# Additive attention masks of the first query block: eight made together on GpSimd, where two were made at each first use

## The chip, the cores and the metric

The kernel runs on one core of one Trainium2 chip. The metric is the device time of one execution in microseconds (us); the kernel before takes 581.28 us, the median of three runs (581.21 to 581.45).

## The reference

Attention over 2 batches, 8 heads, 768 positions and head size 64, followed by two mixture layers on 1536 tokens. Only the attention is touched here. A key is kept for a query when it is one of the first `n_global` (8) positions, or lies at most `n_local` - 1 (95) positions back. A kept key gets a bias that falls with its distance, by a slope of its own for each head:

```python
rel = pos[:, None] - pos[None, :]
is_global = pos[None, :] < int(n_global)
is_local = (rel >= 0) & (rel < int(n_local))
keep = is_global | is_local
dist = np.where(is_global & ~is_local, float(n_local), np.abs(rel).astype(np.float32))
slopes = 2.0 ** (-8.0 * (np.arange(H, dtype=np.float32) + 1) / H)
scores = scores + (-slopes[:, None, None] * dist[None, :, :])[None]
scores = np.where(keep, scores, -1000000000.0)
```

Softmax over the keys and the product with V follow, then `max(x@w1, x@w2, x@w3) @ w_out`, a root-mean-square norm, and `(silu(xn@w_gate) * (xn@w_val)) @ w_out`.

## The kernel before, in words

The attention goes over chunks of two query blocks (a block is 128 queries), and in each chunk over four pairs of heads. A chunk and a pair of heads are a **unit**; 2 x 3 chunks by 4 pairs give 24 units. A query block looks at a window of 232 keys: 96 before it, the 8 global ones, and its own 128. The first query block of a batch has nothing before it and looks at its own 128 keys alone. So there are two widths of mask: narrow (128x128, only for a batch's first query block) and wide (128x232, for all others), each for 8 heads. All depend on a head by one factor, so class `Masks` first makes a common operand for each width on VectorE (lines 706 to 709, tile `mask_mm`, the narrow one first), and each head's mask is that operand times the head's factor, in bf16 (tiles `bias128` and `bias232`, line 715). The first use of a mask makes it, narrow ones on GpSimd, wide ones on VectorE; later units find it made.

`steps` goes over the units with a lead of three: in one step TensorE computes the scores of unit d+3 (line 766), then transposes the weights of unit d+1 (line 807), then multiplies those of unit d with V (line 830), with small filler matmuls in between in the first steps (line 369). For the scores of a unit, `exponents` issues for each query block and each of the two heads a reduction on VectorE (line 779) that adds the mask to the scores, writes the sum and keeps its row minimum, and an exponential on ScalarE (line 783) with its row sum. `normalise` takes the reciprocal of the sums on VectorE (lines 791, 792) and scales the weights on GpSimd (line 797, four instructions a unit).

In the part of the program in which this happens the order on TensorE, VectorE, ScalarE and GpSimd is that in which the code issues the instructions (`manual(FRONT)`); each engine runs its own queue in order. In a step `normalise` of a unit is issued ahead of `exponents` of the next one, and a mask that does not yet exist is issued where `exponents` asks for it:

```python
do(self.normalise, j + LEAD - 1)
do(self.out, j - 1, True)
do(self.scores, j + LEAD)
do(self.transposes, j + 1)
do(self.turned, j + 1, 0)
do(self.exponents, j + LEAD, 0)
```

The score banks have one buffer (`scp`, bufs=1), so the scores of a unit are computed when the reductions of the unit before have read theirs. Transfers are issued by SP's queue. The mixture layers follow; their weights are loaded and split (lines 127 to 168) beside the attention.

Of the kernel before, what the change touches and what calls it, by code (L numbers as in the profile page):

```python
# [13 lines left out]
ALU = mybir.AluOpType  # L14
PSUM = bass.MemoryType.PSUM

P = 128
B, H, S, D = 2, 8, 768, 64
# [11 lines left out]
WIN = NPREV + NG + P  # L30
# [33 lines left out]
SLOPES = [2.0 ** (-8.0 * (h + 1) / H) for h in range(H)]  # L64
# [3 lines left out]
class Later:  # L68
# [3 lines left out]
    def __init__(self):  # L72
        self.now, self.queue = 0, {}

    def __call__(self, steps, fn, *args):
        self.queue.setdefault(self.now + steps, []).append((fn, args))
# [604 lines left out]
class Masks:  # L681
# [3 lines left out]
    def __init__(self, tc, ctx, nlf, ngf):  # L685
        nc = self.nc = tc.nc
        pool = ctx.enter_context(tc.tile_pool(name="mk", bufs=1, side="right"))
        self.out = {n: pool.tile([P, H, n], BF16, name=f"bias{n}") for n in (P, WIN)}
        self.made = set()
        own = NPREV + NG  # L690
        rd = pool.tile([P, 2, WIN], F32, tag="rd", name="mask_rd")
        mm = pool.tile([P, WIN + P], F32, tag="mm", name="mask_mm")
        cg = pool.tile([P, 2, NG], F32, tag="cg", name="mask_cg")
        rel = rd[:, 0]

        kw = {"allow_small_or_imprecise_dtypes": True}
        nc.gpsimd.iota(rel[:, own:], [[-1, P]], base=0, channel_multiplier=1, **kw)
        nc.gpsimd.affine_select(
            rel[:, own:], rel[:, own:], [[-1, P]], ALU.is_ge, FAR, base=0, channel_multiplier=1
        )  # L700
        nc.gpsimd.iota(cg[:, 0], [[1, NG]], base=0, channel_multiplier=0, **kw)
        nc.gpsimd.iota(rel[:, :NPREV], [[-1, NPREV]], base=NPREV, channel_multiplier=1, **kw)
        nc.gpsimd.memset(rel[:, NPREV:own], FAR)
        for n, o in ((P, own), (WIN, 0)):
            m = mm[:, WIN:] if n == P else mm[:, :WIN]
            nc.vector.tensor_scalar(m, rel[:, o:], nlf, MASKED, op0=ALU.is_ge, op1=ALU.mult)
            g = m[:, :NG] if n == P else m[:, NPREV:own]
            nc.vector.scalar_tensor_tensor(out=g, in0=cg[:, 0], scalar=ngf, in1=g, op0=ALU.is_ge, op1=ALU.mult)
            nc.vector.scalar_tensor_tensor(out=m, in0=rel[:, o:], scalar=nlf, in1=m, op0=ALU.min, op1=ALU.add)
        self.parts = {P: mm[:, WIN:], WIN: mm[:, :WIN]}  # L710

    def __call__(self, n, h):
        if (n, h) not in self.made:
            eng = self.nc.gpsimd if n == P else self.nc.vector
            eng.tensor_scalar(self.out[n][:, h, :], self.parts[n], -8.0 * SLOPES[h], 1.0, op0=ALU.mult, op1=ALU.mult)
            self.made.add((n, h))
        return self.out[n][:, h, :]


# [411 lines left out]
```

## Time and profile before

| | |
|---|---|
| median of 3 runs | 581.28 us (581.21 to 581.45) |
| the profiled execution's own time | 581.86 us |
| its span, first to last instruction | 580.0 us |
| TensorE busy | 563.5 us, 97% of the span, 3316 matmuls |
| VectorE busy | 379.6 us, 65% |
| ScalarE busy | 250.9 us, 43% |
| GpSimd busy | 243.2 us, 42%, 301 instructions |
| mean granted clock of TensorE | 0.987 of full speed |

How to read it: the profile records one execution, 1.86 us of whose time lie outside the span. A busy share says how long an engine worked, not whether the end depends on it; that is read from the waits and from the chain of work that ended last. In rows, PE is TensorE, PEld its weight load, DVE VectorE, ACT ScalarE, POOL GpSimd, SP the engine that issues transfers. TensorE's clock has two levels, full (2.4 GHz, shown as 1.00) and half (1.2 GHz, shown as 0.50).

### The profile page before, as it was taken

How to read it: one execution, taken by the hardware profiler on the slowest of the kernel's cores; microseconds unless marked ns; L12 is line 12 of the kernel's file. 1: busy time of each engine (PE TensorE's matmuls, PEld its weight loads, DVE VectorE, ACT ScalarE, POOL GpSimd, SP SyncE). 2: the span in 40 equal slices, each digit the busy share in tenths (PEclk: the TensorE clock that was granted, in tenths of full speed). 3: DMA queues.
4: the chain of work that ended last, by engine and by line, in shares of the span. 5: the costliest groups of instructions: out<-in, count | busy, mean ns of one | idle time of the engine just before them, and what ended most of it. 6: DMA issues, size and time to landing. Idle time of an engine off the chain costs nothing.

```text
span 580.0 us, 9232 instructions
## 1 busy us (share of the span) xinstructions
PE 563.5 (97%) x3316; PEld 510.0 (88%) x3316; DVE 379.6 (65%) x801; ACT 250.9 (43%) x605; POOL 243.2 (42%) x301
## 2 busy tenths in 40 slices
PE   5999999999999999999999999999999999999995
PEld 2677788899999999988899999999999987888884
DVE  4699888826769612156768788888887869762120
ACT  3598676614244201157664444444443435432210
POOL 3456655405145201047647555555565635420000
PEclk9699999999999999999999999999999999999999
DMA  8366655301534400000000222222222104303001
GB/s 301 134 216 199 216 161 180 110 1 49 171 110 152 138 1 0 1 0 2 2 0 1 72 73 74 75 72 73 73 73 73 51 23 146 108 3 127 19 37 42
DMA packets 15895, 48.73 MB, mean 84 GB/s; under 512 B 2016, under 2 KB 2016, under 8 KB 15840
## 3 DMA queue, kind: packets, MB, share of 16 engines
q1 hardware_dynamic: 15840, 48.05, 25.6%
q8 instruction: 28, 0.46, 0.3%
q14 instruction: 27, 0.22, 0.1%
HBM read 44.90 MB, written 3.15 MB: 83 GB/s over the span
## 4 chain that ended last, share of the span: by engine, by line
PE 88%; DVE 5%; ACT 2%; POOL 2%; issue 1%; DMA 1%; SPq 0%; DVEq 0%; POOLq 0%; ACTq 0%
PE q L500 27%; PE mm L379 25%; PE acc L577 16%; PE mo L426 8%; PE sc L766 4%; PE tr L807 3%; PE av L830 3%; ACT s L783 1%; DVE s L779 1%; PE tr L460 1%; DMA qk<-qk 1%; POOL h L550 0%; POOL s L797 0%; POOL op L254 0%; PE idle L369 0%
## 5 line engine op out<-in xcount | busy, mean ns | idle before, releaser
L500 PE MATMUL q<-xb,op 128*128 128x384 f32 x1008 | 175.5, 334 | 0.5 <-POOL op L254 0.5
L500 PEld LDWEIGHTS q<-xb,op 128*128 128x128 f32 x1008 | 174.6, 188 | 0.8 <-POOL op L254 0.8
L379 PE MATMUL mm<-xt,w 128*128 128x384 f32 x864 | 157.5, 338 | 0.0
L379 PEld LDWEIGHTS mm<-xt,w 128*128 128x128 f32 x864 | 148.6, 188 | 2.6 <-issue 2.6
L168 POOL TENSOR_TENSOR w<-x,w 128x512 fp32r<-128x512 f32 x36 | 51.7, 1441 | 74.3 <-ACT w L165 74.2
L797 POOL TENSOR_SCALAR s<-s,rs 128x232 f32<-128x232 f32 (+1 forms) x96 | 43.1, 468 | 42.5 <-DVE rs L792 32.0
L254 POOL TENSOR_TENSOR op<-s,op 128x256 fp32r<-128x256 f32 x48 | 36.9, 781 | 56.7 <-ACT op L253 56.7
L396 DVE TENSOR_TENSOR h<-mm,h 128x384 f32<-128x384 f32 x48 | 26.5, 553 | 46.6 <-PE mm L379 46.4
L426 PE MATMUL mo<-w,rst 128*128 128x512 f32 x216 | 52.1, 395 | 0.0
L783 ACT ACTIVATE s<-s,nmx 128x232 f32<-128x232 f32 (+1 forms) x96 | 44.6, 467 | 15.9 <-DVE nmx L779 15.3
L577 PE MATMUL acc<-w,gst 128*128 128x512 f32 x216 | 49.5, 390 | 1.6 <-POOL w L168 0.8
L577 PEld LDWEIGHTS acc<-w,gst 128*128 128x128 f32 x216 | 40.4, 188 | 10.6 <-POOL w L168 1.2
L577 PE MATMUL acc<-w,st 128*128 128x512 f32 x216 | 49.1, 389 | 0.0
L577 PEld LDWEIGHTS acc<-w,st 128*128 128x128 f32 x216 | 40.5, 188 | 8.4
L426 PEld LDWEIGHTS mo<-w,rst 128*128 128x128 f32 x216 | 39.8, 188 | 8.0
L779 DVE CUSTOM_DVE_ANT_0 s<-sc,bias 128x232 f32<-128x232 f32 (+1 forms) x96 | 32.1, 376 | 12.8 <-PE sc L766 4.6
L517 DVE TENSOR_TENSOR h<-q,h 128x768 f32<-128x768 f32 (+1 forms) x39 | 34.7, 889 | 3.6 <-PE q L500 3.2
L253 ACT CAST op<-s 128x256 fp32r<-128x256 f32 x48 | 18.1, 402 | 41.3 <-DVE s L234 30.8
L766 PE MATMUL sc<-qk 64*128 64x232 f32 (+1 forms) x192 | 28.8, 395 | 7.2 <-DVE nmx L779 6.1
L520 ACT ACTIVATE g<-g 128x768 f32<-128x768 f32 (+1 forms) x26 | 20.8, 798 | 34.8 <-DVE g L517 34.8
L165 ACT CAST w<-x 128x512 fp32r<-128x512 f32 x36 | 22.2, 619 | 26.3 <-DVE x L151 18.0
L766 PEld LDWEIGHTS sc<-qk 64*128 64x128 f32 x192 | 19.0, 202 | 14.2 <-DVE nmx L779 8.3
(102 smaller groups left out, 735.3 us busy)
## 6 DMA issues: line engine op xcount, KB each, us to landing
raw<-wgv SPq DMA_DIRECT2D x24, 512.0 KB, 3.6
raw<-w SPq DMA_DIRECT2D x18, 512.0 KB, 3.8
raw<-wo SPq DMA_DIRECT2D x18, 512.0 KB, 3.6
qk<-qk SPq DMA_DIRECT2D x24, 312.0 KB, 4.0
v<-vwin SPq DMA_DIRECT2D x10, 512.0 KB, 5.1
out<-o SPq DMA_DIRECT2D x12, 256.0 KB, 2.1
v<-vwin SPq DMA_DIRECT2D x2, 256.0 KB, 4.9
gcol<-gcol SPq DMA_DIRECT2D x1, 2.0 KB, 1.6
```

The costliest lines, as they stand in the source:

```text
L168: self.nc.gpsimd.tensor_tensor(out=t[:, 1, :], in0=self.x.pop(i), in1=t[:, 0, :], op=ALU.subtract)
L254: nc.gpsimd.tensor_tensor(out=t[:, 1, :], in0=s, in1=t[:, 0, :], op=ALU.subtract)
L379: self.nc.tensor.matmul(ps, w[:, wi, k * P:(k + 1) * P], x[b][:, k, xi, c0:c0 + C2], start=(i == 0), stop=(i == 3 * KT - 1),)
L396: self.nc.vector.tensor_tensor(out=h, in0=ps, in1=h, op=ALU.max)
L426: self.nc.tensor.matmul(ps, h[:, k % 3, hi, :], w[:, wi, :], start=(k + x == 0), stop=(k == NF1 - 1 and x == 2),)
L500: nc.tensor.matmul(ps, a[:, wi, k * P:(k + 1) * P], self.xb[b][:, j, k, xi, :], start=(i == 0), stop=(i == 5))
L517: nc.vector.tensor_tensor(out=o, in0=ps, in1=x, op=ALU.add)
L577: self.nc.tensor.matmul(ps, of(si), w[:, wi, :], start=(f == LAST[0] and si == 1), stop=(f == LAST[-1] and si == 0 and wi == 0),)
L766: nc.tensor.matmul(sc[j][:, i, :n], qk[r, i * P:(i + 1) * P], qk[r, k0:k0 + n], start=True, stop=True)
L779: nc.vector.tensor_tensor_reduce(out=s[:, j, :n], in0=self.sc[d][j][:, i, :n], in1=self.bias(n, 2 * pr + j), scale=-QK, scalar=3.0e38, op0 ...
L783: nc.scalar.activation(s[:, j, :n], s[:, j, :n], AF.Exp, bias=nmx[:, j:j + 1], scale=-1.0, accum_out=sm[:, i, j:j + 1])
L797: nc.gpsimd.tensor_scalar(s[:, j, :n], s[:, j, :n], rs[:, i, j:j + 1], 1.0, op0=ALU.mult, op1=ALU.mult)
```

## The change

`Masks.__init__` issues all eight narrow masks on GpSimd as soon as the code has issued their common operand, ahead of the wide operand's three instructions. The wide masks are made at their first use on VectorE, as before.

```diff
-        self.made = set()
+        self.made, self.parts = set(), {}
...
             nc.vector.scalar_tensor_tensor(out=m, in0=rel[:, o:], scalar=nlf, in1=m, op0=ALU.min, op1=ALU.add)
-        self.parts = {P: mm[:, WIN:], WIN: mm[:, :WIN]}
+            self.parts[n] = m
+            if n == P:
+                for h in range(H):
+                    self.make(nc.gpsimd, n, h)
+
+    def make(self, eng, n, h):
+        eng.tensor_scalar(self.out[n][:, h, :], self.parts[n], -8.0 * SLOPES[h], 1.0, op0=ALU.mult, op1=ALU.mult)
+        self.made.add((n, h))
 
     def __call__(self, n, h):
         if (n, h) not in self.made:
-            eng = self.nc.gpsimd if n == P else self.nc.vector
-            eng.tensor_scalar(self.out[n][:, h, :], self.parts[n], -8.0 * SLOPES[h], 1.0, op0=ALU.mult, op1=ALU.mult)
-            self.made.add((n, h))
+            self.make(self.nc.vector, n, h)
         return self.out[n][:, h, :]
```

GpSimd's queue from the end of the set-up on, before (`mask_rd` is the distance, `s_0_0` the weights of unit 0 and its first query block, `rs_0` its reciprocals):

```order
L703 MEMSET mask_rd_149 128x8
L715 TENSOR_SCALAR bias128_147<-mask_mm_150 128x128 x2
L797 TENSOR_SCALAR s_0_0_201<-s_0_0_201,rs_0_226 128x128 x2
L797 TENSOR_SCALAR s_0_1_212<-s_0_1_212,rs_0_226 128x232 x2
L715 TENSOR_SCALAR bias128_147<-mask_mm_150 128x128 x2
L797 TENSOR_SCALAR s_1_0_239<-s_1_0_239,rs_1_268 128x128 x2
L797 TENSOR_SCALAR s_1_1_250<-s_1_1_250,rs_1_268 128x232 x2
L715 TENSOR_SCALAR bias128_147<-mask_mm_150 128x128 x2
```

The same place now (lines behind the edit are five higher, and line 715 is 716):

```order
L703 MEMSET mask_rd_149 128x8
L716 TENSOR_SCALAR bias128_147<-mask_mm_150 128x128 x8
L802 TENSOR_SCALAR s_0_0_209<-s_0_0_209,rs_0_232 128x128 x2
L802 TENSOR_SCALAR s_0_1_218<-s_0_1_218,rs_0_232 128x232 x2
L802 TENSOR_SCALAR s_1_0_245<-s_1_0_245,rs_1_272 128x128 x2
L802 TENSOR_SCALAR s_1_1_254<-s_1_1_254,rs_1_272 128x232 x2
```

Three pairs of masks have moved from behind the normalising of units 0, 1 and 2 to the place of the first pair.

VectorE's queue now, from the reciprocal of unit 0 to the second wide mask of unit 1 (rows without an input read out a row minimum; what an instruction waits for stands in brackets):

```order
L797 RECIPROCAL rs_0_232<-rs_0_232 128x4 [waits DVE_49]
L784 ISA s_1_0_245,nmx_1_0_246<-sc0_1_239,bias128_147 128x128 [waits PE_49,Pool_49]
L784 ISA nmx_1_0_246 128x1
L784 ISA s_1_0_245,nmx_1_0_246<-sc1_1_240,bias128_147 128x128 [waits PE_49,Pool_49]
L784 ISA nmx_1_0_246 128x1
L716 TENSOR_SCALAR bias232_148<-mask_mm_150 128x232
L784 ISA s_1_1_254,nmx_1_1_255<-sc0_1_239,bias232_148 128x232 [waits DVE_49]
L784 ISA nmx_1_1_255 128x1
```

Here nothing has moved: the reductions of unit 1 still wait for TensorE and for GpSimd, and the queue reads as before but for line and buffer numbers. So do the queues of ScalarE, TensorE and SP in this part of the program.

## Rows read from the trace of the kernel before

**Rows 1.** Busy time by stretch (start:end, length, each engine's busy us, PEclk, DMA share, GB/s).

```profile
26.00:42.00 16.00, 16.00 (x159) 12.01 (x158) 14.69 (x65) 14.41 (x53) 7.92 (x18) 1.00 0.64 200
```

**Rows 2.** What TensorE waited for, 26 to 60 and 60 to 580: us, times, longest.

```profile
PE sc L766 <- DVE nmx L779: 0.6, 1, 0.6
...
PE acc L577 <- POOL w L168: 0.8, 1, 0.8
```

**Rows 3.** The chain that ended last, 0 to 60: start, us, what.

```profile
10.19 1.60 POOL s L797 x4
11.79 0.28 POOL bias L715
...
13.35 2.20 PE sc L766 x8
15.54 1.47 PE tr L807 x6
17.02 0.23 PE idle L369
...
18.29 2.21 PE sc L766 x8
...
23.99 1.71 PE sc L766 x8
25.70 0.80 PE tr L807 x6
```

**Rows 4.** Timeline: start, us, engine, line, operation, in brackets the idle time before.

```profile
7.63 0.27 DVE L715 TENSOR_SCALAR bias<-mask_mm 128x232 bf16<-128x232 f32 x1
...
9.04 0.88 PE L766 MATMUL sc<-qk 64*128 64x128 f32 x6 [0.15 <-DVE nmx L779]
...
9.84 0.18 DVE L792 RECIPROCAL rs<-rs 128x4 f32<-128x4 f32 x1
...
12.09 0.29 DVE L779 CUSTOM_DVE_ANT_0 s<-sc,bias 128x128 f32<-128x128 f32 x1 [2.08 <-POOL bias L715]
...
14.57 0.17 DVE L791 TENSOR_SCALAR rs<-sm 128x4 f32<-128x4 f32 x1 [0.65 <-ACT s L783]
...
17.03 0.29 DVE L779 CUSTOM_DVE_ANT_0 s<-sc,bias 128x128 f32<-128x128 f32 x1 [2.07 <-PE tr L807]
```

**Rows 5.** GpSimd's timeline from 5 us, and line 797 by form (ns min/median/max).

```profile
6.35 0.70 POOL L715 TENSOR_SCALAR bias<-mask_mm 128x128 bf16<-128x128 f32 x2 [4.01 <-DVE mask_mm L709]
...
16.70 0.57 POOL L715 TENSOR_SCALAR bias<-mask_mm 128x128 bf16<-128x128 f32 x2
...
L715 POOL TENSOR_SCALAR bias<-mask_mm x8: 299/300/317, 6.3 to 22.1; 128x128 bf16<-128x128 f32 x8
L797 POOL TENSOR_SCALAR s<-s,rs x96: 374/462/1141, 10.2 to 114.2; 128x232 f32<-128x232 f32 x80, 128x128 f32<-128x128 f32 x16
```

**Rows 6.** Busy time by stretch again, for the clock (columns as in rows 1).

```profile
10.00:11.60 1.60, 0.24 (x2) 0.00 (x0) 0.01 (x1) 0.00 (x0) 1.41 (x4) 1.00 1.02 415
11.60:13.35 1.75, 0.00 (x1) 0.01 (x1) 1.23 (x8) 0.90 (x5) 0.72 (x3) 0.50 1.03 414
...
18.28:25.20 6.92, 6.92 (x34) 5.24 (x36) 4.38 (x20) 4.37 (x15) 2.20 (x6) 0.50 0.14 47
...
25.20:25.30 0.10, 0.10 (x4) 0.10 (x1) 0.10 (x1) 0.00 (x0) 0.05 (x1) 0.71 0.00 0
```

**Rows 7.** GpSimd and VectorE side by side, at 43.8 and 98.7 us.

```profile
43.78 1.29 POOL L168 TENSOR_TENSOR w<-x,w 128x512 fp32r<-128x512 f32 x1
...
43.95 1.65 DVE L151 SCALAR_TENSOR_TENSOR x<-raw,x 128x512 int32<-128x512 int32 x1
...
98.73 1.82 POOL L797 TENSOR_SCALAR s<-s,rs 128x232 f32<-128x232 f32 x2 [0.44 <-DVE rs L792]
...
99.64 0.67 DVE L145 SCALAR_TENSOR_TENSOR x<-raw,x 128x512 int32<-128x512 int32 x1
```

**Rows 8.** Transfers of q and k, 0 to 40: time to landing.

```profile
DMA to landing us min/median/max: 2.7/4.0/8.1
```

## The prediction

> **What bounds the kernel now.** I read the busy time by stretch first. From 26 us on TensorE works without a gap at the full clock, for instance 16.00 of the 16.00 us from 26 to 42 [rows 1]. Then the list of what TensorE waited for: from 26 us to the end it has one wait of 0.6 us and four that sum to 2.4 us, the longest 0.8 us [rows 2]. (From 42 to 51 us the chain of waits runs through ScalarE and VectorE, but what they do there follows step by step from what came before, so it moves as a whole.) No wait behind 26 us ends at a transfer or at any other event with a time of its own. So the rest of the program moves with its beginning, and what the change is worth is read from the first 26 us alone.
>
> There the chain of waits shows the pattern [rows 3]: GpSimd normalises a unit (four instructions, 1.60 us), then makes a mask (0.28 us), then VectorE's reduction over the scores of the next unit can start, and TensorE's next scores wait for VectorE to empty the score banks. VectorE's own rows show the two waits [rows 4]: 2.08 us before 12.09 and 2.07 us before 17.03. The second is printed as a wait for a transpose; the mask of 16.70 us [rows 5] ends at 16.98, just ahead of 17.03, so it is the mask again. Third, the clock [rows 6]: it falls to 0.50 at 11.60, when TensorE has been idle since 10.24, and comes back at about 25.26 after TensorE has worked without a gap since 18.28. What runs between costs nearly double: six transposes take 1.47 us at the low clock and 0.80 at the high one [rows 3], so each us spent at the low clock costs 0.455 us.
>
> **The change part by part.** I number the units of the first chunk 0 to 3; each has two narrow masks (GpSimd, this change) and two wide ones (VectorE, still made at their first use).
>
> Taken out: three pairs of masks from GpSimd's queue behind the normalising of units 0, 1 and 2. Put in: six masks more behind the first two. A mask is 0.30 us, and followed by another it takes 0.27 to 0.28 of the queue (the pair at 16.70 takes 0.57) [rows 5]. Eight from 6.35 on end by 6.35 + 8 x 0.30 = 8.75, and GpSimd has nothing else until 10.19 [rows 3]: the moved work itself costs nothing, and were that cover gone it would be 6 x 0.28 = 1.7 us. The wait for the first two masks is on the first and second of the eight, in the same place as before, so unit 0 starts at the same time. No transfer moves in any queue, and VectorE, ScalarE, TensorE and SP keep their order.
>
> Term 1, unit 1. VectorE ends its reciprocal at 9.84 + 0.18 = 10.02, and TensorE has the scores ready at 9.04 + 0.88 = 9.92 [rows 4]. The reduction then starts near 10.04 and not at 12.09: **2.05 us earlier**.
>
> Term 2, the wide masks of unit 0. They ran alone in the profile (the first at 7.63, 0.27 us [rows 4]); now GpSimd works beside them until 8.75. No row shows this pair together. The nearest: a VectorE instruction of line 151 whose twin of line 145 takes 0.67 us took 1.65 when it started 0.17 us behind a GpSimd instruction of 1.29 us, that is, it stood until that one was done [rows 7]. So each wide mask waits between nothing and one narrow mask, 0 to 0.30 us; I take the middle, 0.15 each, since the start falls anywhere within a running mask: +0.30 for two (0 to 0.60). They stand on VectorE's path to the reciprocal, so all of it counts.
>
> The Trainium skill, "SBUF — State Buffer", section "Who interferes with whom", says it of a VectorE instruction in a 2-port mode (tensor_scalar can be one) and of one with two SBUF inputs: it and a GpSimd instruction exclude each other for a whole instruction. The trace agrees for line 151. By that rule, with every wide mask caught at the start of a GpSimd instruction, the gain at unit 3 would be the 1.84 us below and not 2.39.
>
> Term 3, the first wide mask of unit 1. Unit 1 now runs beside the normalising of unit 0 (GpSimd instructions of 0.37 to 0.46 us [rows 5]), where before it ran after it: 0 to 0.46, and I take 0.21. The second wide mask there delays only the exponentials (again 0.21).
>
> Scores of unit 2 wait for the third reduction of unit 1, so they start at 13.35 - 2.05 + 0.30 + 0.21 = 11.81. The clock has fallen by then (11.60), so they take the 2.20 us of the row, to 14.01; the transposes of unit 0 follow (1.47, to 15.48), then two filler matmuls of 0.21 each [rows 3]. The transposes need unit 0 normalised: 10.19 + 0.30 + 1.60 + two wide masks of 0.27 in between = 12.6, in time. Scores of unit 3 could start at 15.90, if VectorE is ready: reciprocal of unit 1 at 14.57 - 2.05 + 0.30 + 0.42 = 13.24 [rows 4], reductions of unit 2 from 13.65, the third of them done by 15.05. It is; TensorE is the later. So the scores of unit 3 start at 15.90 where they started at 18.29: **2.39 us earlier**. With no contention at all it is 18.29 - (11.30 + 4.09) = 2.90, about 3.1 with the first 0.3 us at the high clock; with every wide mask waiting a whole GpSimd instruction, 18.29 - (12.36 + 4.09) = 1.84.
>
> From there TensorE has no gap, before and now. The operands are there: the blocks of q and k of units 0 to 3 are the first large transfers in SP's queue, and one takes at most 8.1 us to land [rows 8]; 15.9 leaves nearly twice that. What is late next is TensorE itself.
>
> Term 4, the clock's return, the largest unknown. Its rows are one event, so I bound it by what stood before it. If it comes at the same place in the work (early in the scores of unit 4, 23.99 before), the gain stays 2.4. If it comes after the same length of gapless work (25.26 - 18.28 = 6.98), it comes at 11.81 + 6.98 = 18.8, 4.1 us before that place, and saves 4.1 x 0.455 = 1.85 more: 4.25. If it comes at the same moment, 25.26, the work of 2.4 us runs at the low clock and 2.4 x 0.455 = 1.1 is lost: 1.3. I take 2.8, nearer to the first: the gapless stretch begins earlier now, but with the same short matmuls of the narrow units, and the wide ones still come late in it.
>
> Sum: the profiled execution took 581.86 us, 1.86 more than its span of 580.0; 581.86 - 2.8 = 579.06. The median of the three runs is 581.28, 0.58 lower, so 581.28 - 2.8 = **578.5 us**. The range: 3.1 and 1.85 together give 576.3, rounded to 576.2; 1.84 with the clock at the same moment (1.84 x 0.455 = 0.84 lost) gives 1.0, so 580.3.
>
> **The rivals.** *The clock never falls.* If unit 2's scores begin ahead of 11.60, TensorE's idle time ahead of it shrinks from 1.36 us to 1.0, and the clock may hold. Then TensorE is no longer the bound, but the loop from reduction to reciprocal to the next reduction: 14.57 - 12.09 = 2.48, and 0.4 for the reciprocal and 0.42 for contention, 3.3 a unit. The reductions of unit 4 come at 10.34 + 3 x 3.3 = 20.2, and the scores that they read were done at 25.70 before: 5.5 earlier, 575.8. Against it: by term 2 the scores come after 11.60, when the gap is as long as before. Chance 0.07.
>
> *GpSimd keeps the operands for its whole group.* Then a wide mask waits not for one instruction but for the end of the group. Unit 0 loses 8.75 - 7.63 = 1.12, unit 1 some 1.25, unit 2 some 1.3; scores of unit 2 start at 13.7, those of unit 3 at 17.85, 0.4 before the old time: 580.9, no difference that can be told. Against it: at 99.64 a VectorE instruction of line 145 (two SBUF operands) ran its usual 0.67 us among two of GpSimd's normalising instructions, and these took 1.82 together instead of 2 x 0.46 [rows 5, 7]: it got in between and held up GpSimd. Chance 0.09. Another 0.02 for a gain that is swallowed later by a wait that the profile does not show, and 0.02 for the forecast's own edge below the bound of 0.2%.
>
> *The low clock lasts longer* (the other side). TensorE's gaps move, and the work between 11.8 and 20 us is made of short matmuls; if these do not bring the clock back, each us of delay behind 22.9 costs 0.455. The gain of 2.4 is used up if it returns at 22.9 + 2.4 / 0.455 = 28.2, and the kernel is slower by over 0.2% from 30.8 on. Half as long again as the 13.66 us of before ends at 32.1: 2.4 - 9.2 x 0.455 = -1.8, so 583.1. Against it: work without a gap brought it back in 7 us, and the wide scores of unit 4 come at about 21.6 now. Chance 0.04.
>
> That the change does not do what it says I leave out: the order of GpSimd's queue shows the eight together, and unit 1's first reduction waits for the third of them alone.
>
> **How the numbers follow.** A change of 0.2% is 1.2 us, about what a measurement of this kernel can tell from none. Forecast 0.78, of it 0.76 with a gain above that; faster 0.76 + 0.07 = 0.83, the same 0.09 + 0.02 + 0.02 = 0.13, slower 0.04.
>
> **What would show it.** Right: one row of eight masks on GpSimd from about 6.35 to 9; no wait of VectorE for a mask behind 8 us; the reduction of unit 1 near 10.3, the scores of unit 2 near 11.8 and of unit 3 near 15.9; the wide masks of units 0 and 1 at 0.3 to 0.7 us and not 0.28 throughout; the clock's fall at about 11.6 and its return between 18.8 and 25.3. Wrong: wide masks of over 1 us, a reduction of unit 1 that still starts after 11.5, or a clock that returns after 26.

## The result and the profile after

The changed kernel takes 575.68 us, the median of four runs (575.32 to 576.32), the kernel before beside it 581.35 (581.21 to 581.45): 5.67 us less, a ratio of 0.9904 with a 95% interval of 0.9887 to 0.9921. Faster was forecast, but by 2.8 us, with a range down to 576.2; the time lies 0.5 us below it. A second measurement (after_again below) gave 575.69 against 581.62, 0.9894 (0.9877 to 0.9910). The two profiled executions lie 6.54 us apart, more than the medians: that of the kernel before is 0.5 us above its median, that of the changed one 0.4 below.

| | before | after |
|---|---|---|
| the profiled execution's own time | 581.86 us | 575.32 us |
| its span | 580.0 us | 573.5 us |
| TensorE busy | 563.5 us, 97% | 561.3 us, 98% |

First VectorE's queue after the change: its timeline from 7 to 17 us (start, us, engine, line, operation; in brackets the idle time before and what ended it).

```profile
7.70 0.27 DVE L716 TENSOR_SCALAR bias<-mask_mm 128x232 bf16<-128x232 f32 x1
...
8.33 0.28 DVE L716 TENSOR_SCALAR bias<-mask_mm 128x232 bf16<-128x232 f32 x1
...
10.02 0.29 DVE L784 CUSTOM_DVE_ANT_0 s<-sc,bias 128x128 f32<-128x128 f32 x1
...
10.45 0.31 DVE L716 TENSOR_SCALAR bias<-mask_mm 128x232 bf16<-128x232 f32 x1
...
11.12 0.44 DVE L716 TENSOR_SCALAR bias<-mask_mm 128x232 bf16<-128x232 f32 x1
...
12.97 0.29 DVE L784 CUSTOM_DVE_ANT_0 s<-sc,bias 128x128 f32<-128x128 f32 x1
...
16.48 0.29 DVE L784 CUSTOM_DVE_ANT_0 s<-sc,bias 128x128 f32<-128x128 f32 x1 [0.30 <-PE sc L771]
```

The reductions of units 1, 2 and 3 start at 10.02, 12.97 and 16.48. Before they started at 12.09 and 17.03 [rows 4], and that of unit 3 at 22.09, in a row of the trace of before that the prediction did not use:

```profile
22.09 0.29 DVE L779 CUSTOM_DVE_ANT_0 s<-sc,bias 128x128 f32<-128x128 f32 x1 [2.19 <-POOL bias L715]
```

So there were three waits for a mask, not two, and all three are gone. The lead over the kernel before grows unit by unit: 2.07, 4.06, 5.61 us.

GpSimd after the change (its timeline; the second row is unit 0's normalising):

```profile
6.42 2.73 POOL L716 TENSOR_SCALAR bias<-mask_mm 128x128 bf16<-128x128 f32 x8 [4.08 <-DVE mask_mm L709]
10.26 1.62 POOL L802 TENSOR_SCALAR s<-s,rs 128x128 f32<-128x128 f32 x4 [1.11 <-DVE rs L797]
```

The eight masks stand together and end at 9.15, 1.11 us ahead of the next work.

The clock, by stretches between its changes (start:end, length, busy us and number on PE, PEld, DVE, ACT and POOL, PEclk, DMA share, GB/s):

```profile
9.31:12.72 3.41, 2.23 (x17) 1.32 (x16) 2.27 (x13) 2.40 (x10) 1.62 (x4) 1.00 1.02 416
12.72:16.13 3.41, 3.41 (x18) 2.49 (x16) 3.02 (x15) 2.46 (x10) 1.62 (x4) 0.50 1.03 413
16.13:26.00 9.87, 9.87 (x95) 7.28 (x93) 9.03 (x42) 8.24 (x32) 5.28 (x13) 1.00 0.53 164
```

It is at 0.50 from 12.72 to 16.13 alone, 3.41 us, where before it was so from 11.60 to 25.26, 13.66 us [rows 6]. And the chain of waits (start, us, what) runs from 12.05 on through TensorE:

```profile
12.05 0.96 PE sc L771 x6
13.02 1.47 PE tr L812 x6
...
14.92 1.49 PE sc L771 x8
16.41 0.81 PE tr L812 x6
...
17.33 0.81 PE av L835 x12
...
18.36 1.02 PE sc L771 x8
```

Scores of unit 3 come at 14.92, those of unit 4 at 18.36, 3.4 and 5.6 us earlier than before [rows 3].

Two explanations are left by this. **Theory 1**: before the change units 1 to 3 were paced by a loop that holds no matmul that matters (reduction, exponentials, reciprocal, normalising, mask), and the low clock lay hidden in it; three waits of 2.08, 2.07 and 2.19 us, 6.3 in all, leave it. **Theory 2**, the prediction's: behind 18.3 us TensorE was the bound, each us at the low clock cost 0.455 us, and what came beyond 2.4 us is the shorter stretch at the low clock. They differ in what the clock does alone: by the second, holding it up without the change gives a good part of the gain; by the first, nothing.

### The profile page after: what moved, and what is told of

Read it like the earlier page. It is cut to its first block, busy times and chain, and to the rows that moved or that the text cites. A ratio compares the mean times of both kernels' runs of the same rounds, so it can differ in the third digit from the quotient of the medians.

```text
span 573.5 us, 9229 instructions
## 1 busy us (share of the span) xinstructions
PE 561.3 (98%) x3316; PEld 508.2 (89%) x3316; DVE 379.5 (66%) x801; ACT 250.4 (44%) x605; POOL 241.2 (42%) x301
## 4 chain that ended last, share of the span: by engine, by line
PE 91%; DVE 4%; POOL 2%; ACT 1%; issue 1%; DMA 1%; SPq 0%; DVEq 0%; ACTq 0%
PE q L500 28%; PE mm L379 27%; PE acc L577 16%; PE mo L426 8%; PE tr L812 4%; PE sc L771 4%; PE av L835 4%; PE tr L460 1%; DVE s L784 1%; DMA ni<-nn 1%; ACT s L788 0%; POOL h L550 0%; POOL op L254 0%; PE idle L369 0%; ACT xb L464 0%
## 5 line engine op out<-in xcount | busy, mean ns | idle before, releaser
L165 ACT CAST w<-x 128x512 fp32r<-128x512 f32 x36 | 22.2, 619 | 26.6 <-DVE x L151 18.3
L771 PE MATMUL sc<-qk 64*128 64x232 f32 (+1 forms) x192 | 27.6, 388 | 2.9 <-DVE nmx L784 1.8
L517 DVE TENSOR_TENSOR g<-q,h 128x768 f32<-128x768 f32 (+1 forms) x13 | 11.6, 894 | 26.9 <-PE q L500 26.9
```

What stands on the lines that cost most here:

```text
L517: nc.vector.tensor_tensor(out=o, in0=ps, in1=x, op=ALU.add)
L771: nc.tensor.matmul(sc[j][:, i, :n], qk[r, i * P:(i + 1) * P], qk[r, k0:k0 + n], start=True, stop=True)
```

## Experiments

All are compared with the kernel before on the same chip, which took 581.35 to 581.62. "Low clock" is the stretch at 0.50 in the profiled execution, from its first rise on and within the first 26 us; the starts are read from the profiled execution too.

| kernel | us (runs) | reductions of units 1, 2, 3, 4 start at | low clock |
|---|---|---|---|
| before | 581.35 (4) | 12.09, 17.03, 22.09, 25.65 | 11.60 to 25.26 |
| before_fill | 581.39 (10) | 12.16, 17.10, 22.14, 25.35 | none from 10.1 on |
| before_cold | 581.31 (10) | 12.09, 17.01, 22.05, 25.50 | until 25.0 |
| before_wide | 580.36 (10) | 12.16, 16.80, 21.57, 24.37 | 11.2 to 21.5 |
| four_early | 579.84 (9) | 10.42, 15.69, 20.73, 23.94 | 14.0 to 20.9 |
| six_early | 577.78 (4) | 10.33, 13.09, 18.25, 21.46 | 13.4 to 20.2 |
| dve_lazy | 577.87 (4) | 11.03, 14.63, 18.40, 21.98 | 12.6 to 19.4 |
| after_cold | 577.55 (4) | 10.36, 13.93, 17.49, 22.89 | until 22.5 |
| pair_ahead | 576.21 (4) | 10.42, 13.19, 16.13, 19.36 | none from 10.2 on |
| after | 575.68 (4) | 10.02, 12.97, 16.48, 19.55 | 12.72 to 16.13 |
| after_again | 575.69 (4) | 9.96, 13.29, 17.11, 20.52 | 10.93 to 17.76 |
| after_fill | 575.04 (4) | 10.41, 13.22, 16.16, 19.39 | none from 10.3 on |
| wide_only | 573.75 (5) | 10.40, 12.91, 15.43, 18.25 | none from 10.1 on |
| wide_ahead | 573.76 (4) | 10.12, 12.63, 15.15, 17.97 | none from 4.7 on |

### The clock alone, in the kernel before: before_fill

```diff
+    def fill(self, n):
+        for x in range(n):
+            self.nc.tensor.matmul(self.bank(f"fill_{x}"), self.zeros[:, :P], self.zeros, start=True, stop=True)
...
                         if r < WARMR:
                             body.keep_warm(r)
+                        if part == 1:
+                            body.fill({1: 10, 2: 10, 3: 6}.get(r, 0))
```

> The kernel before, masks still made in pairs at their first use, with 26 more filler matmuls (128x512) in the gaps that TensorE has in front of the scores of units 2, 3 and 4, so that its clock stays up. Theory 1 (before the change, units 1 to 3 are paced by a loop that holds no matmul that matters: reduction, exponentials, reciprocal, GpSimd's normalising, GpSimd's mask, 5 us a unit at either clock, and the low clock is hidden in it): the reductions of units 1 to 3 stay within 0.3 us of 12.1, 17.0 and 22.1, and the time is 580.3 to 581.8 us. Theory 2 (what the change gave beyond 2.4 us came from the shorter stretch at the low clock alone): the clock held up by fillers gives that without the change, 577.5 to 579 us.

581.39 us, a ratio of 0.9997 (0.9988 to 1.0007): no difference in the medians. The stretches show the clock up and the gaps filled:

```profile
10.00:11.60 1.60, 1.60 (x10) 0.68 (x9) 0.10 (x1) 0.00 (x0) 1.32 (x4) 1.00 1.01 412
11.60:13.35 1.75, 1.42 (x7) 0.44 (x5) 1.15 (x8) 0.85 (x4) 0.80 (x3) 1.00 1.02 413
18.30:25.20 6.90, 6.29 (x43) 3.79 (x44) 4.38 (x20) 4.40 (x16) 2.18 (x6) 1.00 0.18 50
```

and VectorE's timeline the same three waits at the same times:

```profile
12.16 0.29 DVE L784 CUSTOM_DVE_ANT_0 s<-sc,bias 128x128 f32<-128x128 f32 x1 [2.06 <-PE fill L370]
17.10 0.29 DVE L784 CUSTOM_DVE_ANT_0 s<-sc,bias 128x128 f32<-128x128 f32 x1 [2.06 <-POOL bias L720]
22.14 0.29 DVE L784 CUSTOM_DVE_ANT_0 s<-sc,bias 128x128 f32<-128x128 f32 x1 [2.18 <-POOL bias L720]
```

(The first is printed as a wait for a filler; the reduction has no part in that, and the mask's end is as near.) The chain of waits of this kernel holds no matmul between the reduction at 12.4 and that at 22:

```profile
14.85 0.19 DVE rs L797
...
15.21 1.59 POOL s L802 x4
16.79 0.28 POOL bias L720
...
17.10 0.04 DVE s L784
```

So the first half of theory 2 falls: the clock held up from 10 to 26 us is worth nothing in the median while the mask is in the loop. Against the profiled execution of the kernel before (581.86) it is worth 0.5 us: the loop lets the scores of unit 4 start at 23.51, where TensorE at the low clock came to them at 23.99 [rows 3].

```profile
23.51 0.66 PE sc L771 x2
```

### The other way: before_cold and after_cold

```diff
-WARM = 10
+WARM = 0
...
-                        if r < WARMR:
+                        if 3 <= r < WARMR:
                             body.keep_warm(r)
```

The same edit in the kernel before and in the changed one.

> The kernel before without the ten warm-up matmuls and without the fillers of the first three steps, so that TensorE starts at the low clock and stays there longer. Theory 1 (the loop through GpSimd hides the low clock up to the scores of unit 4): reductions of units 1 to 3 within 0.4 us of 12.1, 17.0 and 22.1 again; what is lost comes behind them, 581.0 to 583.5 us in all. Theory 2 (TensorE at the low clock bounds these units already): each of the us from 5 to 11 that is now at the low clock costs 0.45, 584 us or more.

> The changed kernel with the same cut: no warm-up matmuls, no fillers in the first three steps. Theory 1: without the mask in the loop TensorE at the low clock is the bound (scores 2.2, transposes 1.5, values 1.5 us a unit), so scores of unit 4 start near 20.6 and not 18.3, and the gain over the kernel before with the same cut shrinks from 5.7 to 2.5 to 4 us: 578 to 580 us. Were the clock of no weight: 575.7 us again.

before_cold: 581.31 us, 0.9993 (0.9983 to 1.0002). The clock's first rise is recorded at 25.0 us, and until then the column prints 1.00, since nothing was recorded before it; that it was low the durations show. Here the chain of waits, where the scores take 2.20 us as in [rows 3]:

```profile
13.35 2.20 PE sc L766 x8
15.55 1.49 PE tr L807 x6
17.03 0.02 DVE s L779
...
18.27 2.20 PE sc L766 x8
20.47 1.48 PE tr L807 x6
```

Time and reductions lie where theory 1 put them. In the kernel before two bounds stood side by side: from the scores of unit 3 to those of unit 4 TensorE at the low clock works 5.7 us (18.29 to 23.99 [rows 3]), and the mask's loop alone, with the clock up, takes 5.2 (18.35 to 23.51 in before_fill). Taking away one of them alone, as before_fill did, or letting the low clock stand from the start, as here, changes next to nothing.

after_cold: 577.55 us, 0.9928 (0.9912 to 0.9945), 1.9 more than the change and 0.4 below the expected range; its profiled execution, the longest of the four, took 578.79 (the others 577.45 to 577.58). Its chain is TensorE's from 12 us on:

```profile
12.01 2.20 PE sc L771 x8
14.21 1.47 PE tr L812 x6
15.68 2.09 PE sc L771 x8
17.77 1.47 PE tr L812 x6
...
19.45 1.48 PE av L835 x12
...
21.26 1.59 PE sc L771 x8
```

Scores of unit 4 come at 21.26, 0.6 later than expected. The medians of before_cold and after_cold are 3.8 us apart, within the 2.5 to 4 expected; the profiled executions 2.9, near the 2.4 that the prediction had worked out for a clock that returns in the scores of unit 4, as it does here. So without the mask in the loop TensorE at the low clock is the bound and the clock has a price, 1.9 us in the median: the second half of theory 2 holds for the changed kernel. With the mask in the loop the price is next to nothing. The gain is not the sum of the two; it takes the mask out of the loop for the clock to count.

### Pair by pair: four_early and six_early

The changed kernel with `for h in range(4)` (or 6) in place of `range(H)`, the other narrow masks on GpSimd at their first use as before.

> The change done half: four narrow masks (units 0 and 1) made at once, the pairs of units 2 and 3 at their first use as before. Theory 1: each pair that leaves the loop is worth 2.0 us, so one of three gives 579.0 to 579.6 us; the reduction of unit 1 starts near 10.0 and those of units 2 and 3 follow 5 us apart. Theory 2: the clock falls and returns nearly as before, and what is gained at unit 1 is the 2 us at most, or nearly all of the 5.7 us when the clock comes back early (576 us), but nothing in proportion to the pairs.

> Six narrow masks (units 0 to 2) made at once, the pair of unit 3 at its first use as before. Theory 1 (each pair taken out of the loop is worth about 2 us, one by one; four early gave 1.6): two of three gives 3.4 to 4.2 us, 577.2 to 578.0 us; the reduction of unit 3 alone still stands some 5 us behind that of unit 2. Theory 2 (the gain comes with the clock): no steps, 576 or 579 us.

Four: 579.84, 0.9968 (0.9958 to 0.9978), 1.6 us; six: 577.78, 0.9936 (0.9919 to 0.9952), 3.6 us. With eight, 5.67. The table has the steps: behind the last early pair the next reduction stands 5.2 to 5.3 us after the one before it (13.09 to 18.25, 10.42 to 15.69), and in four_early the following one 5.0, though the clock stands elsewhere in each. Four fell 0.2 us short of its range. In its profiled execution the first reduction starts at 10.42 and not 10.02: it waits for the scores of unit 1, which took 1.95 us (in the changed kernel 1.40), since the clock rose only at 10.61, at their end. All kernels of the table with 10.3 to 10.4 show this wait of 0.3 us.

### The place in the queue: pair_ahead

```diff
+            do(self.masks, j + LEAD)
             do(self.normalise, j + LEAD - 1)
...
+    def masks(self, d):
+        x, pr, first, n = self.unit(d, 0)
+        if first:
+            for j in range(2):
+                self.bias(n, 2 * pr + j)
```

> The kernel before with one thing changed: each pair of narrow masks is issued on GpSimd ahead of the normalising of the unit before, not behind it; never more than four stand together. Theory 1 (the place in GpSimd's queue is all): as the change, 575.2 to 576.7 us. Rival (making them all in the idle time at the start matters, since a pair in the loop still costs GpSimd 0.57 us there): 1 to 2 us more than the change, 576.7 to 577.7 us.

576.21 us (575.15 to 577.18), 0.9912 (0.9894 to 0.9930), within theory 1's range. Its profiled execution is the one of 575.15, with the clock up throughout; the three longer ones had a mean granted clock of 0.991 to 0.992 against its 0.997. A pair ahead of the normalising gives what eight at once give, to within the spread of the runs. It was the order of two things in one queue, not the amount of work in it.

### On the other engine: dve_lazy

```diff
-            eng = self.nc.gpsimd if n == P else self.nc.vector
+            eng = self.nc.vector
```

> The kernel before with the narrow masks made at first use on VectorE, like the wide ones, and none on GpSimd. Theory 1: the wait for GpSimd is gone as with the change, but two masks of about 0.2 us stand in VectorE's loop in each of units 1 to 3: 1.3 us more than the change, 576.5 to 577.5 us. If GpSimd being freed of the work counts more than the queue's order, no worse than the change.

577.87 us, 0.9935 (0.9918 to 0.9951): 0.4 above the range, 2.2 more than the change. Two more masks on VectorE, 0.20 to 0.22 us each, made the units 3.6 to 3.8 us long where the change has 3.0 to 3.5, and the low clock lasted 6.8 us. The reduction of unit 1 already starts 1.0 us later than in the changed kernel (11.03), with the clock still up: unit 0 has two such masks as well, which the expectation left out. How the rest of the 2.2 us divides between masks and clock was not separated.

### What the clock still costs: after_fill and after_again

after_fill is the changed kernel with `body.fill({1: 4}.get(r, 0))`: four fillers in front of the scores of unit 2. after_again is the changed kernel unaltered.

> The changed kernel with four more filler matmuls (128x512) in front of the scores of unit 2, where TensorE still has a gap of 1.2 us in the profile, so that the clock does not fall there. If the one stretch of 3.4 us at the low clock that is left costs what its rows say (0.455 us per us at most, part of it beside the loop): 574.3 to 575.5 us. If the loop on VectorE and ScalarE is the bound there by now: 575.2 to 576.0 us, no gain. Where the clock has not yet risen, the four cost 0.8 us.

> The changed kernel once more, on the same chip as the run beside it, for the spread of its time and of the clock's stretches: 575.3 to 576.4 us, with single executions about 1 us apart where the kernel with four fillers had 0.2.

after_fill: 575.04 us, all four between 574.92 and 575.10; 0.9885 (0.9869 to 0.9902). after_again: 575.69, between 575.41 and 576.29, and its profiled execution is that of 576.29, with a longer low stretch than the first profile's:

```profile
10.93:17.76 6.83, 6.55 (x27) 4.64 (x28) 4.96 (x25) 4.05 (x16) 3.38 (x10) 0.50 1.02 405
```

6.83 us against 3.41, and 576.29 against 575.32: 1.0 us for 3.4 us, some 0.3 a us. What is left of the clock in the changed kernel is about 0.65 us in the median, and fillers take it away. The gain is then 581.35 - 575.04 = 6.31 us, and the three waits were 2.08 + 2.07 + 2.19 = 6.34. With the clock up in both kernels, before_fill against after_fill, it is 6.35. That these agree so closely is in part chance: by the reductions of unit 4 after_fill is 6.0 us ahead of before_fill (19.39 against 25.35), and the rest comes at about 92 us, as told under why the prediction was wrong.

### The wide masks: before_wide, wide_only and wide_ahead

```diff
             do(self.exponents, j + LEAD, 1)
+            do(self.wide, j + LEAD + 1)
...
+    def wide(self, d):
+        for j in range(2):
+            self.bias(WIN, 2 * (d % NPAIR) + j)
```

The two wide masks of the next unit go behind a unit's reductions on VectorE's queue. before_wide is the kernel before with this, wide_only the changed one, wide_ahead the changed one with the four fillers too.

> The kernel before, narrow masks as before, with the two wide masks of the next unit made on VectorE right behind a unit's reductions instead of between them. Theory 1 (units 1 to 3 are paced by the loop of reductions, exponentials, reciprocal, normalising and narrow mask): two wide masks of 0.3 us leave the loop in each of three units, 1.5 to 2.0 us less, 579.4 to 580.0 us, whatever the clock does. Theory 2 (TensorE at the low clock bounds them): no change, 581.2 to 581.6 us.

> The changed kernel with the wide masks moved and without the four fillers. The loop is shorter by 0.6 us a unit if it still paces: with the fillers that gave 573.76 us. If the clock holds by itself, since the gap in front of the scores of unit 2 shrinks: 573.7 to 574.4 us; if it falls, TensorE at the low clock takes the gain back: 574.6 to 575.7 us.

> The changed kernel with the four fillers, and with the two wide masks of the next unit made on VectorE right behind a unit's reductions, where VectorE waits 0.65 us for the last exponential, and not between its reductions. If VectorE's loop still paces units 1 to 3: up to 0.3 us a unit, 574.0 to 574.8 us. If TensorE does (15.38 of 16.00 us busy from 10 to 26): no change against 575.04, 574.8 to 575.2 us.

before_wide: 580.36 us, 0.9982 (0.9972 to 0.9992), 1.2 us less where 1.5 to 2.0 were expected of theory 1 and nothing of theory 2: outside both ranges, nearer to the first. Three of its ten executions took 581.55 to 581.61, the others 580.10 to 580.85. The units became 4.64 and 4.77 us long where they were 4.94 and 5.06, since the exponentials took the place of the reductions in the loop:

```profile
12.49 1.83 ACT s L787 x8
...
14.90 1.60 POOL s L801 x4
16.50 0.28 POOL bias L715
...
16.80 0.04 DVE s L783
```

wide_only: 573.75 us (four of five between 573.70 and 574.24, one 575.84), 0.9870 (0.9851 to 0.9888); wide_ahead: 573.76 (573.69 to 574.11), 0.9864 (0.9847 to 0.9880). Both beat the change by 1.9 us and are the fastest kernels here, 7.8 us below the kernel before beside them (581.57 and 581.62). wide_ahead gave 1.3 more than the fillers alone, against an expected 0.2 to 1.0. In the changed kernel VectorE's loop, not TensorE, was the pace of these units once the clock held: their distance fell from 2.8 to 2.9 us (after_fill) to 2.5. In wide_only the clock held without fillers in the profiled execution; that of 575.84 has no profile, but its mean granted clock is 0.991 where the other four have 0.997 to 0.998, so it fell there.

## Why the prediction was wrong

The direction was right, the wait that the change removes, and for the most part the place. The size was off, 2.8 us for 5.67. Of TensorE's four waits behind 60 us in the kernel before, three (0.8, 0.8 and 0.5 us) stand unchanged. The fourth is gone: the scores at 102.41 waited 0.3 us for VectorE there. The chain leads back to a reduction that waits for GpSimd's normalising (four instructions): in the kernel before it starts at 92.94, with the fourth at its end (91.26 to 93.03), in the changed one at 86.36, with the third (of 85.03 to 86.79). That takes VectorE's lead between the two traces from 6.22 to 6.57 us, outside the first units. The kernels that make the last pair of masks in the loop (six_early, four_early) still have TensorE's wait; why the reduction waits for one instruction less was not followed. Here are the two reductions in VectorE's timelines, before and after:

```profile
92.94 0.40 DVE L779 CUSTOM_DVE_ANT_0 s<-sc,bias 128x232 f32<-128x232 f32 x1 [1.57 <-POOL s L797]
86.36 0.40 DVE L784 CUSTOM_DVE_ANT_0 s<-sc,bias 128x232 f32<-128x232 f32 x1 [1.22 <-POOL s L802]
```

**Masks, GpSimd, first reduction: right.** Eight masks in one row, 6.42 to 9.15 (about 9 forecast); no wait for a mask on VectorE; the reduction of unit 1 is 2.07 us earlier (2.05).

**Term 2, too large: 0.30 us, measured none.** The wide masks of unit 0 took 0.27 and 0.28 us, the first 0.27 as in [rows 4], while GpSimd made masks beside them. It was GpSimd that lost time: its eight took 2.73 us, where eight at the 0.27 to 0.28 of an undisturbed pair are 2.2. About half of that it lost before the first wide mask, beside VectorE's work on the wide operand.

**Term 3, too large: 0.21 us, measured 0.03** (0.31 for the first wide mask of unit 1; the second, 0.44, lost 0.16). With term 2 that put the scores of unit 2 at 11.26 and not at 11.81. These two terms are 0.5 us of the miss.

**The clock's fall, 0.5 us more.** The prediction had it at 11.60, ahead of the scores of unit 2, and gave them 2.20 us, to 14.01. It fell at 12.72; the scores, with a wait of 0.31 us in between, ended at 13.02. So the scores of unit 3 came at 14.92 and not at 15.90.

**The step that failed: "What is late next is TensorE itself", and term 4, the clock's return, that rested on it.** TensorE has indeed no gap from the scores of unit 3 on, before and after. But the prediction took that gapless work for the only bound (6.92 of 6.92 us busy, [rows 6]) and ended its sum of waits there. In the kernel before a second bound of nearly the same length stood beside it: the third mask's wait, 2.19 us at 22.09, was in the trace and was left out. So the kernel before could not serve as the measure for what the clock costs: before_fill shows that its low clock cost nothing there in the median, and 0.5 us against the profiled execution. And term 4 treated the clock as an event with a place of its own, put its return between 18.8 and 25.3, and gave 0.4 us for it (2.8 against 2.39). It came back at 16.13 and 17.76 in the two profiled executions of the changed kernel, ahead of the earliest bound. The gaps that had kept TensorE idle in front of it (10.24 to 13.35 before) came from the waits that the change removes. From the scores of unit 3 to those of unit 4 the changed kernel takes 3.44 us (3.92 in after_again) and not the 5.7 of before; that is 2.3 us (1.8) where the term had 0.4. Both had to go for that, the third wait and the low clock: six_early, which keeps the third wait, is 2.1 us slower than the change, and after_cold, which keeps the low clock to 22.5 us, 1.9. What decides when the clock returns is not shown; the runs show that it never fell where fillers took the gaps away.

**The rivals.** The one without a low clock gave 575.8 us, and the time came out there, but that is luck: its condition did not hold, since the clock fell in both profiles, for a shorter time, and with the clock up (after_fill) the kernel takes 575.04. Its working was the better model all the same, since it asked how long the loop on VectorE and ScalarE takes. GpSimd did not keep the operands for a group (no wide mask beyond 0.44 us, 0.50 in after_again), and the low clock did not last longer.

**The range.** Its lower end, 576.2, joined the best cases of terms that all took the low-clock work of the kernel before as their measure; the three waits that the trace shows, 6.3 us, would have put the end at 575.0.

## What to carry to other kernels

A busy engine is the bound only if nothing else takes as long beside it: follow the loop of waits of the other engines through the same stretch, and count each of its waits, also where the busiest engine shows no gap. When an engine's clock fell while it waited, and stays up once its gaps are filled (before_fill), do not carry the place or the cost of the low clock over into a kernel that no longer has the wait. In a queue that runs in order, issue work whose inputs are ready ahead of work that waits for the step before.

## What the runs showed of the hardware that was not expected

The low stretch differs between executions of the same kernel: 12.72 to 16.13 and 10.93 to 17.76 for the changed one, 1.0 us apart in time. The other executions fit: the two of 576.3 us have a mean granted clock of 0.991, the six of 575.3 to 575.8 one of 0.995 or 0.996. The kernel before has a spread too, of another kind: 47 of its 57 executions took 581.19 to 581.96 us and ten 582.81 to 583.08, at a mean clock of 0.986 to 0.991 in both groups. No long one was profiled, so what they lose is open; none of the 20 executions of before_fill and before_cold was longer than 581.84.

Side by side with GpSimd's masks VectorE's one-input instructions (the wide masks) lost nothing, and GpSimd's train of eight lost 0.5 us in all; side by side with GpSimd's normalising (f32, in place) they lost up to 0.16 us of 0.28, in after_again up to 0.23 (0.50 at 13.93). The rule of the Trainium skill that was cited, "SBUF — State Buffer", section "Who interferes with whom", lets the instruction that is issued first hold the other up. The trace agrees with that for the mask of 0.44 us at 11.12, which began inside a normalising instruction of GpSimd. For the wide masks of unit 0 it decides nothing: each began only in the last 0.06 to 0.07 us of a GpSimd mask (at 7.70, against 7.48 + 0.29).
